# Linear attention into a sine-activated MLP on one core: first loads reordered, weight casts placed by hand, attention steps on one-bank PSUM tiles

## The chip, the cores and the metric

The kernel runs on one core of a Trainium2 chip. The metric is device time in microseconds, the median of several executions. TensorE (PE, with its weight loads PEld) multiplies matrices into PSUM, VectorE (DVE) and ScalarE (ACT) read PSUM and SBUF, GpSimd (POOL) works in SBUF only, and SyncE (SP) issues transfers. Each engine takes its instructions in the order in which the program lists them for it.

## The reference

```python
q_s = softmax(q, axis=-1)                    # per row, 8 batches, 8 heads, 576 x 64
k_s = softmax(k, axis=2)                     # along the sequence
kv  = einsum('bhsd,bhse->bhde', k_s, v)
x   = einsum('bhsd,bhde->bhse', q_s, kv)     # -> x: (4608, 512)
h   = x @ w_in                               # w_in: (512, 2048)
g   = h + sin(alpha * h)**2 / (alpha + 1e-9)
out = g @ w_out                              # w_out: (2048, 512), out: (4608, 512)
```

## The kernel before

Tokens are split in two ways. Attention goes by batch: 8 batches of 576 rows, held as 9 groups (J) of 64. The MLP goes by tile t: 9 tiles of 512 tokens. Tile t needs the attention output (tile `xT`, features on partitions) of batches up to t, except that tile 8 needs batch 7 at most.

A tile is 16 steps `ni`, one for each 128 of the 2048 hidden units. In step ni, `mm_h` runs four matmuls of 512 columns into a PSUM tile `hp` (a ring of four one-bank tiles), and `snake` runs Sin on ACT, the square on ACT ("A"), POOL ("P") or DVE ("D"), and a DVE operation that adds hp and frees its PSUM tile. The second product, `mm_o`, is 64 matmuls for each tile. It runs one tile later: `o_stream(t-1)` feeds some of these matmuls behind each step of tile t, by the count `want`. Four times a tile `evac_o` copies a finished accumulator out and stores it.

Attention of a batch is: `exp_q`, `exp_k` (ACT, two operations each), `cast_v` (two casts to bf16 into `vb`), `norm_q` (DVE row sums and reciprocal, then one multiply into `qn`), `kv_mm` (36 small matmuls of `ke` and `vb` into `kvp`), `kv_norm` (DVE, into `kvb`), three `q_transpose` (six PE transposes into `tp`, one copy into `qT`), and four `attn_out` (two matmuls into `xp`, two copies into `xT`). The tiles kvp, tp and xp share the pool `ps_a`, which has one buffer of two banks. Batches 0 and 1 run on their own, ahead of tile 0 and ahead of tile 1. Batch t+1 is spread over the steps of tile t for t from 1 to 6: exponentials, casts and the loads of the next batch behind step 1, `norm_q` with its multiply on POOL behind step 4, `kv_mm` behind 5, `kv_norm` behind 6, the transposes behind 8 to 10, `attn_out` behind 12 to 15. Each of these stands behind that step's `snake` in program order, so on DVE the copies queue behind the add of the step.

All weights and inputs are float32 in memory and are loaded into a ring of six staging tiles (tag "st"): q, k, v of batch 0, then four chunks of w_in, four of w_out, then the later batches. A chunk of w_in comes as two transfers of 64 partitions, one from SP's queue and one from ACT's. The w_in chunks are cast to bf16 on DVE, one ahead of every fourth step of tile 0 (line 266), behind all adds that were listed earlier. The w_out chunks are cast on POOL behind the whole of tile 0 (line 277). In tile 0 `mm_o` runs on its own, with four accumulators at once.

Of the kernel before, what the change touches and what calls it, by code (L numbers as in the profile page):

```python
# [15 lines left out]
F32 = mybir.dt.float32  # L16
# [7 lines left out]
def kernel(  # L24
# [20 lines left out]
    J = 9  # L45
# [18 lines left out]
    ps_a = ctx.enter_context(tc.tile_pool(name="ps_a", bufs=1, space=bass.MemoryType.PSUM))  # L64
# [40 lines left out]
    def load_win(c):  # L105
        st = stage.tile([128, 4, 512], F32, name="st_w", tag="st")
        for x, eng in ((0, nc.sync), (1, nc.scalar)):
            eng.dma_start(out=st[64 * x:64 * x + 64], in_=win_v[x][:, :, c * 512:(c + 1) * 512])
        wst["i", c] = st
# [61 lines left out]

    def q_transpose(b, g):
# [33 lines left out]
    def snake(t, ni, hp, sq):  # L206
# [174 lines left out]
```

## Time and profile before

| | |
|---|---|
| median of 3 runs | 439.46 us (438.34 to 441.27) |
| profiled execution | 441.32 us, its span 439.0 us |
| mean granted TensorE clock | 0.891 of full speed |
| PE busy | 317.4 us, 72% of the span |
| ACT busy | 232.6 us, 53% |
| DVE busy | 210.1 us, 48% |
| POOL busy | 58.1 us, 13% |

The span is the stretch that the trace covers; 2.3 us of the profiled execution lie around it. Busy shares are averages over stages that differ much, so the rows below go by stage.

### The profile page before, as it was taken

The page shows a single profiled execution, that of the slowest core. Times are in us where ns is not written, and L with a number is a line of the kernel's source. Part 1 is how long each engine was busy: PE and PEld are TensorE (multiplying, and loading weights), DVE is VectorE, ACT ScalarE, POOL GpSimd, SP SyncE. Part 2 cuts the span into 40 slices and gives each one's busy share as a digit, 9 for nine tenths or more (in the row PEclk, how much of TensorE's full clock was granted, in tenths as well). Part 3 has the DMA queues.
Part 4 walks back from the last instruction along what each step waited for, and adds up shares of the span by engine and source line. Part 5 has one row for each costly group of instructions (what it writes and reads, how often), then busy time and mean ns, then how long its engine had stood idle before and what let it go on. Part 6 is the DMA issues. An engine that isn't in the chain of part 4 may idle for free.

```text
span 439.0 us, 4398 instructions
## 1 busy us (share of the span) xinstructions
PE 317.4 (72%) x1621; PEld 147.8 (34%) x1649; DVE 210.1 (48%) x331; ACT 232.6 (53%) x326; POOL 58.1 (13%) x40
## 2 busy tenths in 40 slices
PE   0055566915754689588877969795889588999995
PEld 0032122403322334234333424342434243444442
DVE  0545543073255634554646284628453665554531
ACT  0505337000861459357825974595569456777730
POOL 0000006300213020500140032005000300000000
PEclk9999668965765889899969997997899899999999
DMA  7994234669080001118210911191111111212133
GB/s 262 298 266 167 97 111 166 261 185 342 5 317 1 0 2 23 24 24 276 103 28 16 341 54 24 32 339 25 26 24 25 24 24 26 48 24 50 28 69 72
DMA packets 22821, 46.43 MB, mean 106 GB/s; under 512 B 1792, under 2 KB 1808, under 8 KB 22800
## 3 DMA queue, kind: packets, MB, share of 16 engines
q1 hardware_dynamic: 21712, 44.06, 32.1%
q10 hardware_dynamic: 1088, 2.10, 1.7%
q8 instruction: 13, 0.21, 0.2%
q14 instruction: 8, 0.07, 0.0%
HBM read 36.71 MB, written 9.44 MB: 105 GB/s over the span
## 4 chain that ended last, share of the span: by engine, by line
PE 42%; ACT 21%; DVE 15%; issue 10%; POOL 6%; DMA 2%; POOLq 1%; SPq 0%; ACTq 0%; DVEq 0%
PE hp L202 19%; PE op L219 16%; ACT s L208 9%; POOL qn L144 5%; ACT s L210 4%; DVE g L215 3%; DVE xT L192 3%; PE tp L180 3%; ACT ke L121 3%; DVE qs L141 2%; ACT L121 2%; DMA st_k<-in_k_dram 2%; ACT qe L121 2%; ACT L208 2%; PE hp L219 2%
## 5 line engine op out<-in xcount | busy, mean ns | idle before, releaser
L215 DVE SCALAR_TENSOR_TENSOR g<-s,inva_sb,hp 128x512 bf16<-128x512 f32 x144 | 106.3, 745 | 158.9 <-ACT s L210 139.4
L202 PE MATMUL hp<-xT,win 128*128 128x512 bf16 x569 | 165.7, 422 | 20.0 <-DVE win L266 12.0
L208 ACT ACTIVATE s<-hp,alpha_sb 128x512 f32<-128x512 f32 x144 | 98.2, 684 | 121.4 <-PE hp L202 106.8
L219 PE MATMUL op<-wout,g 128*128 128x512 bf16 x523 | 140.6, 392 | 4.7 <-POOL wout L277 3.8
L202 PEld LDWEIGHTS <-win 128*128 128x128 bf16 x576 | 61.4, 108 | 96.4 <-issue 30.2
L219 PEld LDWEIGHTS <-g 128*128 128x128 bf16 x576 | 57.0, 101 | 73.3 <-issue 15.4
L210 ACT ACTIVATE s<-s 128x512 f32<-128x512 f32 x126 | 79.4, 630 | 4.0
L180 PE MATMUL tp<-identb,qn 128*128 128x128 bf16 x144 | 17.0, 278 | 62.1 <-POOL qn L144 22.0
L144 POOL TENSOR_TENSOR qn<-qe,qs 128x2304 bf16<-128x2304 bf16 x6 | 24.3, 4047 | 171.4 <-ACT s L210 160.6
L180 PEld LDWEIGHTS <-qn 128*128 128x128 bf16 x144 | 13.4, 127 | 72.2 <-DVE qn L144 27.7
L224 DVE COPY o<-op 128x512 f32<-128x512 f32 x34 | 22.9, 676 | 29.4 <-PE op L219 29.4
L188 PE MATMUL xp<-qT,kvb 128*128 128x256 bf16 x64 | 15.2, 324 | 23.7 <-DVE xT L192 19.1
L192 ACT CAST xT<-xp 128x256 bf16<-128x256 f32 (+1 forms) x8 | 2.8, 402 | 51.7 <-PE xp L188 51.7
L141 DVE TENSOR_REDUCE qs<-qe 128x36 f32<-128x2304 bf16 x8 | 20.4, 2546 | 12.3 <-ACT qe L121 12.3
L212 POOL TENSOR_TENSOR s<-s 128x512 f32<-128x512 f32 x10 | 10.4, 1041 | 116.6 <-ACT s L208 116.6
L192 DVE CAST xT<-xp 128x256 bf16<-128x256 f32 (+1 forms) x56 | 22.8, 448 | 5.8 <-PE xp L188 5.8
L188 PEld LDWEIGHTS <-kvb 128*128 128x128 bf16 x64 | 6.6, 106 | 34.6 <-issue 27.1
L121 ACT ACTIVATE qe<-st_q 128x1152 bf16<-128x1152 f32 x16 | 17.7, 1155 | 0.1
L121 ACT ACTIVATE ke<-st_k 128x1152 bf16<-128x1152 f32 x16 | 17.6, 1146 | 0.0
L181 DVE COPY qT<-tp 128x768 bf16<-128x768 bf16 x24 | 13.3, 554 | 8.0 <-PE tp L180 8.0
L121 ACT ACT_TABLE_LOAD x8 | 10.3, 1283 | 11.3 <-DMA st_k<-in_k_dram 11.2
L135 POOL CAST vb<-st_v 128x1152 bf16<-128x1152 f32 x14 | 15.8, 1162 | 0.0
(26 smaller groups left out, 83.3 us busy)
## 6 DMA issues: line engine op xcount, KB each, us to landing
out_dram<-o SPq DMA_DIRECT2D x72, 128.0 KB, 2.4
st_q<-in_q_dram SPq DMA_DIRECT2D x7, 1152.0 KB, 5.6
st_k<-in_k_dram SPq DMA_DIRECT2D x7, 1152.0 KB, 9.2
st_v<-in_v_dram SPq DMA_DIRECT2D x7, 1152.0 KB, 10.3
st_w<-in_moe_w_out_dram SPq DMA_DIRECT2D x4, 1024.0 KB, 8.0
st_w<-in_moe_w_in_dram ACTq DMA_DIRECT2D x4, 512.0 KB, 9.5
st_w<-in_moe_w_in_dram SPq DMA_DIRECT2D x4, 512.0 KB, 16.1
st_q<-in_q_dram SPq DMA_DIRECT2D x2, 576.0 KB, 6.8
```

The lines of the kernel that those rows point to most:

```text
L121: nc.scalar.activation(dst[:, :, ii * 128:(ii + 1) * 128].rearrange("p j (x d) -> p x j d", x=2), src[:, ii::2], AX.Exp)
L141: nc.vector.tensor_reduce(qs, qe3, axis=AXL.X, op=ALU.add)
L144: eng.tensor_tensor(qn.rearrange("p j (i d) -> p (j i) d", i=4), qe3, qs.unsqueeze(2).to_broadcast([128, J * 4, D]), op=ALU.mult)
L180: nc.tensor.transpose(tp[:, jj, ii], qn[:, 3 * g + jj, ii * 128:(ii + 1) * 128], identb)
L188: nc.tensor.matmul(op[:, half, 0:(j1 - j0) * P], kt[:, hp, :], qT[:, j0:j1, ii, e * 64:(e + 1) * 64], start=True, stop=True)
L192: eng(xT[:, hp, c0:c0 + (j1 - j0) * P], op[:, half, 0:(j1 - j0) * P])
L202: nc.tensor.matmul(hp, win[:, ki, ni * 128:(ni + 1) * 128], xT[:, ki, t * MF:(t + 1) * MF], start=(ki == 0), stop=(ki == 3))
L208: nc.scalar.activation(s, hp, AX.Sin, scale=alpha_sb[:, ni:ni + 1])
L210: nc.scalar.activation(s, s, AX.Square)
L215: nc.vector.scalar_tensor_tensor(G[t][:, ni], in0=s, scalar=inva_sb[:, ni:ni + 1], in1=hp, op0=ALU.mult, op1=ALU.add)
L219: nc.tensor.matmul(acc, G[t][:, ni, j * 128:(j + 1) * 128], wout[:, ni, :], start=(ni == 0), stop=(ni == nN - 1))
L224: eng(o, acc)
```

## The change

The first loads all go through SP's queue, in the order q, k, v, the four w_in chunks, the four w_out chunks, batch 1. The w_in casts move to POOL (chunks 0 and 2) and DVE (1 and 3), and three of the four w_out casts move into tile 0. `norm_q` can be done in halves on two engines; for batch 0 both halves go to DVE, for batch 1 one to DVE and one to POOL. `cast_v` of batch 0 moves to POOL. The pool ps_a gets two buffers, and kvp becomes two one-bank tiles, xp one such tile per half. In batches 0 and 1 the copies of the transposes go to ACT, and the two halves of `attn_out` to DVE and ACT. The row sums of batch 1 move ahead of tile 0's output copies. `snake` is split into `sine` and `combine`, and the attention steps of a tile stand between `mm_h` and these. In the tiles the exponentials, `norm_q` and `cast_v`, in this order, stand behind step 0, `kv_mm` and `kv_norm` in step 4, the transposes in 6 to 8, `attn_out` in 9 to 12, and step 0 takes 20 matmuls of `o_stream`.

```diff
-    ps_a = ctx.enter_context(tc.tile_pool(name="ps_a", bufs=1, space=bass.MemoryType.PSUM))
+    ps_a = ctx.enter_context(tc.tile_pool(name="ps_a", bufs=2, space=bass.MemoryType.PSUM))
...
     def load_win(c):
         st = stage.tile([128, 4, 512], F32, name="st_w", tag="st")
-        for x, eng in ((0, nc.sync), (1, nc.scalar)):
-            eng.dma_start(out=st[64 * x:64 * x + 64], in_=win_v[x][:, :, c * 512:(c + 1) * 512])
+        for x in range(2):
+            nc.sync.dma_start(out=st[64 * x:64 * x + 64], in_=win_v[x][:, :, c * 512:(c + 1) * 512])
         wst["i", c] = st
...
-    def norm_q(b, eng):
+    def norm_q(b, engs):
+
         qe = A["qe", b]
-        qs = small.tile([128, J * 4], F32, name="qs")
-        qe3 = qe.rearrange("p j (i d) -> p (j i) d", i=4)
-        nc.vector.tensor_reduce(qs, qe3, axis=AXL.X, op=ALU.add)
-        nc.vector.reciprocal(qs, qs)
         A["qn", b] = qn = att1.tile([128, J, 4 * D], BF16, name="qn")
-        eng.tensor_tensor(qn.rearrange("p j (i d) -> p (j i) d", i=4), qe3,
-                          qs.unsqueeze(2).to_broadcast([128, J * 4, D]), op=ALU.mult)
-
-    def kv_mm(b, ii, first):
-        if first:
-            A["kvp", b] = ps_a.tile([128, 2, 512], F32, name="kvp", tag="a")
+        qs = small.tile([128, J, 4], F32, name="qs")
+        n = len(engs)
+        w = 4 // n
+        for h in range(n):
+            cols = slice(h * w * D, (h + 1) * w * D)
+            src = qe[:, :, cols].rearrange("p j (i d) -> p j i d", i=w)
+            dst = qn[:, :, cols].rearrange("p j (i d) -> p j i d", i=w)
+            part = qs[:, :, h * w:(h + 1) * w]
+            nc.vector.tensor_reduce(part, src, axis=AXL.X, op=ALU.add)
+            nc.vector.reciprocal(part, part)
+            engs[h].tensor_tensor(dst, src, part.unsqueeze(3).to_broadcast([128, J, w, D]), op=ALU.mult)
+
+    def kv_mm(b, ii):
+        if ii == 0:
+            A["kvp", b] = [ps_a.tile([128, 512], F32, name="kvp", tag="a") for _ in range(2)]
         kvp, ke, vt = A["kvp", b], A["ke", b], vb[b % 2]
         for j in range(J):
             for e in range(2):
                 r = slice(64 * e, 64 * e + 64)
-                nc.tensor.matmul(kvp[:, e, ii * 130:(ii + 1) * 130],
+                nc.tensor.matmul(kvp[e][:, ii * 130:(ii + 1) * 130],
                                  ke[r, j, ii * 128:(ii + 1) * 128],
                                  vt[r, j, ii * 130:(ii + 1) * 130],
                                  start=(j == 0), stop=(j == J - 1))
 
     def kv_norm(b):
-        kvp = A["kvp", b]
         A["kvb", b] = kt = kvb[b % 2]
         kvr = small.tile([128, 2, 2], F32, name="kvr")
-        for x in range(2):
-            r = slice(64 * x, 64 * x + 64)
-            src = kvp[r, :, 0:260].rearrange("p e (ii c) -> p e ii c", ii=2)
-            nc.vector.reciprocal(kvr[r], src[:, :, :, x * 65 + 64])
-            nc.vector.tensor_tensor(
-                kt[r].rearrange("p (ii e) c -> p e ii c", e=2)[:, :, :, x * 64:(x + 1) * 64],
-                src[:, :, :, x * 65:x * 65 + 64],
-                kvr[r].unsqueeze(3).to_broadcast([64, 2, 2, D]), op=ALU.mult)
-
-    def q_transpose(b, g):
+        for e in range(2):
+            for x in range(2):
+                r = slice(64 * x, 64 * x + 64)
+                src = A["kvp", b][e][r, 0:260].rearrange("p (ii c) -> p ii c", ii=2)
+                nc.vector.reciprocal(kvr[r, e], src[:, :, x * 65 + 64])
+                nc.vector.tensor_tensor(
+                    kt[r, e::2, x * 64:(x + 1) * 64],
+                    src[:, :, x * 65:x * 65 + 64],
+                    kvr[r, e].unsqueeze(2).to_broadcast([64, 2, D]), op=ALU.mult)
+
+    def q_transpose(b, g, eng):
...
-        nc.vector.tensor_copy(qT[:, 3 * g:3 * g + 3], tp)
-
-    def attn_out(b, hp, eng):
+        eng(qT[:, 3 * g:3 * g + 3], tp)
+
+    def attn_out(b, hp, half, eng):
         ii, e = divmod(hp, 2)
         qT, kt = A["qT", b], A["kvb", b]
-        op = ps_a.tile([128, 2, 512], F32, name="xp", tag="a")
-        for half, (j0, j1) in enumerate(((0, 4), (4, 9))):
-            nc.tensor.matmul(op[:, half, 0:(j1 - j0) * P], kt[:, hp, :],
-                             qT[:, j0:j1, ii, e * 64:(e + 1) * 64], start=True, stop=True)
-        for half, (j0, j1) in enumerate(((0, 4), (4, 9))):
-            c0 = (J * b + j0) * P
-            eng(xT[:, hp, c0:c0 + (j1 - j0) * P], op[:, half, 0:(j1 - j0) * P])
+        j0, j1 = ((0, 4), (4, 9))[half]
+        n = (j1 - j0) * P
+        xp = ps_a.tile([128, 512], F32, name="xp", tag="a")
+        nc.tensor.matmul(xp[:, 0:n], kt[:, hp, :], qT[:, j0:j1, ii, e * 64:(e + 1) * 64],
+                         start=True, stop=True)
+        c0 = (J * b + j0) * P
+        eng(xT[:, hp, c0:c0 + n], xp[:, 0:n])
...
-    def snake(t, ni, hp, sq):
+    def sine(t, ni, hp, sq):
         s = spool.tile([128, MF], F32, name="s")
         nc.scalar.activation(s, hp, AX.Sin, scale=alpha_sb[:, ni:ni + 1])
         if sq == "A":
@@ -212,6 +218,9 @@
             nc.gpsimd.tensor_tensor(s, s, s, op=ALU.mult)
         else:
             nc.vector.tensor_tensor(s, s, s, op=ALU.mult)
+        return s
+
+    def combine(t, ni, hp, s):
         nc.vector.scalar_tensor_tensor(G[t][:, ni], in0=s, scalar=inva_sb[:, ni:ni + 1],
                                        in1=hp, op0=ALU.mult, op1=ALU.add)
...
+    ACT_CP, DVE_CP = nc.scalar.copy, nc.vector.tensor_copy
     nc.sync.dma_start(out=alpha_rows, in_=moe_alpha.rearrange("(no ni) -> no ni", ni=128))
     load("q", q, 0, halves=True)
     load("k", k, 0, halves=True)
     load("v", v, 0, halves=True)
+    for c in range(4):
+        load_win(c)
     make_identity(nc, ident)
-    nc.vector.tensor_copy(identb, ident)
+    DVE_CP(identb, ident)
     for n in range(2):
         nc.vector.memset(vb[n].rearrange("p j (i c) -> p j i c", i=4)[:, :, :, D:D + 1], 1.0)
         nc.vector.memset(kvb[n], 0.0)
-    load_win(0)
-    load_win(1)
-    load_win(2)
+    tpa = ps_a.tile([128, nN], F32, name="tpa", tag="a")
+    nc.tensor.transpose(tpa, alpha_rows, ident[0:nN, 0:nN])
+    DVE_CP(alpha_sb, tpa)
+    nc.vector.reciprocal(inva_sb, alpha_sb)
+
     exp_q(0)
     exp_k(0)
-    norm_q(0, nc.vector)
-    load_win(3)
-    tpa = ps_a.tile([128, nN], F32, name="tpa", tag="a")
-    nc.tensor.transpose(tpa, alpha_rows, ident[0:nN, 0:nN])
-    nc.vector.tensor_copy(alpha_sb, tpa)
-    nc.vector.reciprocal(inva_sb, alpha_sb)
+    norm_q(0, [nc.vector, nc.vector])
+    cast_v(0, nc.gpsimd)
+    for c in range(4):
+        load_wout(c)
     for g in range(3):
-        q_transpose(0, g)
-    cast_v(0, nc.vector)
+        q_transpose(0, g, ACT_CP)
     for ii in range(2):
-        kv_mm(0, ii, ii == 0)
+        kv_mm(0, ii)
     kv_norm(0)
+
+    def cast_win(c, eng):
+        eng(win[:, :, c * 512:(c + 1) * 512], wst["i", c])
+
+    def cast_wout(c, eng):
+        eng(wout[:, 4 * c:4 * c + 4, :], wst["o", c])
+
+    cast_win(0, nc.gpsimd.tensor_copy)
     for hp in range(4):
-        attn_out(0, hp, nc.vector.tensor_copy if hp % 2 == 0 else nc.scalar.copy)
-
-
+        attn_out(0, hp, 0, DVE_CP)
+        attn_out(0, hp, 1, ACT_CP)
+    cast_win(1, DVE_CP)
+
+
+    load_batch(1)
     SQ0 = "APADAPADPADAPADP"
     for ni in range(nN):
-        if ni % 4 == 0:
-            c = ni // 4
-            nc.vector.tensor_copy(win[:, :, c * 512:(c + 1) * 512], wst["i", c])
-            if c < 2:
-                load_wout(c + 2)
-            elif c == 2:
-                load("q", q, 1)
-                load("k", k, 1)
-            else:
-                load("v", v, 1)
         hp = mm_h(0, ni)
-        snake(0, ni, hp, SQ0[ni])
-    for c in range(4):
-        nc.gpsimd.tensor_copy(wout[:, 4 * c:4 * c + 4, :], wst["o", c])
+        if ni == 2:
+            cast_win(2, nc.gpsimd.tensor_copy)
+        if ni == 6:
+            cast_win(3, DVE_CP)
+        if ni in (7, 10, 13):
+            cast_wout(ni // 3 - 2, nc.gpsimd.tensor_copy)
+        combine(0, ni, hp, sine(0, ni, hp, SQ0[ni]))
+    cast_wout(3, nc.gpsimd.tensor_copy)
 
     accs = [ps_o.tile([128, dm], F32, name="op", tag="o") for _ in range(2)]
     accs += [ps_h.tile([128, dm], F32, name="hp", tag="h") for _ in range(2)]
@@ -282,21 +297,20 @@
         for j in range(4):
             mm_o(0, j, ni, accs[j])
     exp_q(1)
+    norm_q(1, [nc.vector, nc.gpsimd])
     exp_k(1)
-    load("q", q, 2)
-    load("k", k, 2)
+    cast_v(1, nc.gpsimd)
     for j in range(4):
-        evac_o(0, j, accs[j], nc.vector.tensor_copy)
-    norm_q(1, nc.vector)
-    cast_v(1, nc.gpsimd)
-    load("v", v, 2)
+        evac_o(0, j, accs[j], DVE_CP)
+    load_batch(2)
     for g in range(3):
-        q_transpose(1, g)
-    kv_mm(1, 0, True)
-    kv_mm(1, 1, False)
+        q_transpose(1, g, ACT_CP)
+    kv_mm(1, 0)
+    kv_mm(1, 1)
     kv_norm(1)
     for hp in range(4):
-        attn_out(1, hp, nc.vector.tensor_copy if hp % 2 == 0 else nc.scalar.copy)
+        attn_out(1, hp, 0, DVE_CP)
+        attn_out(1, hp, 1, ACT_CP)
...
         for ni in range(nN):
             hp = mm_h(t, ni)
-            snake(t, ni, hp, "A" if t > 1 else SQ0[ni])
             if b is not None:
-                if ni == 1:
-                    exp_q(b)
-                    exp_k(b)
-                    cast_v(b, nc.gpsimd)
-                    if b + 1 < B:
-                        load_batch(b + 1)
-                elif ni == 4:
-                    norm_q(b, nc.gpsimd)
-                elif ni == 5:
-                    kv_mm(b, 0, True)
-                    kv_mm(b, 1, False)
-                elif ni == 6:
+                if ni == 4:
+                    kv_mm(b, 0)
+                    kv_mm(b, 1)
                     kv_norm(b)
-                elif 8 <= ni < 11:
-                    q_transpose(b, ni - 8)
-                elif ni >= 12:
-                    attn_out(b, ni - 12, nc.vector.tensor_copy)
+                elif 6 <= ni < 9:
+                    q_transpose(b, ni - 6, DVE_CP)
+                elif 9 <= ni < 13:
+                    attn_out(b, ni - 9, 0, DVE_CP)
+                    attn_out(b, ni - 9, 1, DVE_CP)
+            combine(t, ni, hp, sine(t, ni, hp, "A" if t > 1 else SQ0[ni]))
+            if b is not None and ni == 0:
+                exp_q(b)
+                exp_k(b)
+                norm_q(b, [nc.gpsimd])
+                cast_v(b, nc.gpsimd)
+                if b + 1 < B:
+                    load_batch(b + 1)
             if os is not None:
-                if b is not None:
-                    want = 20 + 16 * ni // 5 if ni >= 1 else 3
-                    want = min(64, want)
-                else:
-                    want = 4 * (ni + 1)
-                while done < want:
+                want = 20 + 11 * ni // 4 if b is not None else 4 * (ni + 1)
+                while done < min(64, want):
                     next(os)
                     done += 1
```

## Rows read from the trace of the kernel before

**Rows 1.** Windows by stage: busy us of each engine (count), granted clock, DMA share, GB/s
```profile
0.00:35.20 35.20, 7.36 (x63) 4.97 (x65) 13.81 (x24) 7.25 (x10) 0.70 (x6) 1.00 0.96 279
35.20:73.40 38.20, 23.21 (x62) 8.29 (x63) 17.86 (x23) 18.94 (x27) 7.06 (x7) 0.78 0.35 117
73.40:89.00 15.60, 15.51 (x63) 6.56 (x63) 0.51 (x1) 2.66 (x3) 7.71 (x5) 0.89 0.62 227
89.00:111.90 22.90, 7.26 (x64) 4.94 (x65) 11.98 (x18) 0.91 (x3) 0.00 (x0) 0.55 0.77 253
111.90:156.80 44.90, 26.36 (x127) 11.58 (x129) 22.55 (x37) 23.63 (x32) 13.32 (x10) 0.73 0.22 79
156.80:365.20 208.40, 169.24 (x935) 80.52 (x949) 110.80 (x183) 137.03 (x190) 29.36 (x14) 0.93 0.24 76
365.20:439.00 73.80, 68.47 (x312) 30.92 (x316) 32.60 (x47) 42.21 (x64) 0.00 (x0) 1.00 0.20 47
```
**Rows 2.** Timeline of PE in tile 4: start, us, instruction, [idle before <- releaser]
```profile
243.31 4.48 PE L219 MATMUL op<-wout,g 128*128 128x512 bf16 x20
...
263.56 0.82 PE L180 MATMUL tp<-identb,qn 128*128 128x128 bf16 x6 [4.40 <-POOL qn L144]
...
276.74 0.41 PE L188 MATMUL xp<-qT,kvb 128*128 128x256 bf16 x2 [1.20 <-DVE xT L192]
...
283.19 0.38 PE L202 MATMUL hp<-xT,win 128*128 128x512 bf16 x1 [0.53 <-DVE xT L192]
```
**Rows 3.** Windows of tile 4, behind its longest PE wait
```profile
263.50:268.40 4.90, 4.84 (x21) 2.63 (x22) 0.83 (x2) 0.96 (x2) 2.21 (x3) 0.50 0.00 0
268.40:275.00 6.60, 6.44 (x35) 3.07 (x34) 3.77 (x6) 4.13 (x7) 0.00 (x0) 0.97 0.17 40
```
**Rows 4.** Timeline of ACT from the start
```profile
0.73 10.40 ACTq L108 DMA_DIRECT2D st_w<-in_moe_w_in_dram  x3
11.16 1.28 ACT L121 ACT_TABLE_LOAD   x1 [11.16 <-DMA st_k<-in_k_dram]
```
**Rows 5.** Timeline of PE, second chunk of w_in in tile 0
```profile
44.87 6.30 PE L202 MATMUL hp<-xT,win 128*128 128x512 bf16 x16 [3.85 <-DVE win L266]
```
**Rows 6.** Timelines of DVE and PE between tiles 0 and 1
```profile
92.28 0.69 DVE L224 COPY o<-hp 128x512 f32<-128x512 f32 x1 [1.91 <-DMA out_dram<-o]
...
98.49 0.82 PE L180 MATMUL tp<-identb,qn 128*128 128x128 bf16 x6 [9.39 <-DVE qn L144]
```
**Rows 7.** The page's DMA issues: count, KB each, median us from issue to landing
```profile
st_q<-in_q_dram SPq DMA_DIRECT2D x2, 576.0 KB, 6.8
```
**Rows 8.** Windows of the first loads (last two columns: DMA share, GB/s)
```profile
6.00:12.00 6.00, 0.00 (x0) 0.00 (x0) 0.00 (x0) 0.84 (x1) 0.00 (x0) 1.00 1.05 390
24.00:30.00 6.00, 2.89 (x39) 2.18 (x39) 3.38 (x8) 0.00 (x0) 0.00 (x0) 1.00 1.08 199
```
**Rows 9.** Groups by line and shape: busy, mean ns of one | idle before it
```profile
L208 ACT ACTIVATE s<-hp,alpha_sb 128x512 f32<-128x512 f32 x144 | 98.2, 684 | 121.4 <-PE hp L202 106.8 <-DVE g L215 13.6 <-PE xp L188 0.5
...
L121 ACT ACTIVATE qe<-st_q 128x1152 bf16<-128x1152 f32 x16 | 17.7, 1155 | 0.1
...
L277 POOL CAST wout<-st_w 128x2048 bf16<-128x2048 f32 x4 | 7.4, 1891 | 0.0
L167 DVE TENSOR_TENSOR kvb<-kvp,kvr 64x256 bf16<-64x256 f32 x16 | 6.8, 422 | 0.5
```
**Rows 10.** Timelines of ACT, DVE and POOL in tile 4
```profile
244.23 0.63 ACT L210 ACTIVATE s<-s 128x512 f32<-128x512 f32 x1
...
246.17 2.22 ACT L121 ACTIVATE qe<-st_q 128x1152 bf16<-128x1152 f32 x2
...
256.33 2.54 DVE L141 TENSOR_REDUCE qs<-qe 128x36 f32<-128x2304 bf16 x1
...
259.46 4.05 POOL L144 TENSOR_TENSOR qn<-qe,qs 128x2304 bf16<-128x2304 bf16 x1 [35.48 <-ACT s L210]
263.45 2.26 POOL L135 CAST vb<-st_v 128x1152 bf16<-128x1152 f32 x2
```

More of the change, by code (lines that the diff above doesn't have):

```diff
@@ L238 @@
         nc.vector.memset(kvb[n], 0.0)
-    load_win(0)
-    load_win(1)
-    load_win(2)
+    tpa = ps_a.tile([128, nN], F32, name="tpa", tag="a")
+    nc.tensor.transpose(tpa, alpha_rows, ident[0:nN, 0:nN])
+    DVE_CP(alpha_sb, tpa)
+    nc.vector.reciprocal(inva_sb, alpha_sb)
     exp_q(0)
     exp_k(0)
-    norm_q(0, nc.vector)
-    load_win(3)
-    tpa = ps_a.tile([128, nN], F32, name="tpa", tag="a")
-    nc.tensor.transpose(tpa, alpha_rows, ident[0:nN, 0:nN])
-    nc.vector.tensor_copy(alpha_sb, tpa)
-    nc.vector.reciprocal(inva_sb, alpha_sb)
+    norm_q(0, [nc.vector, nc.vector])
+    cast_v(0, nc.gpsimd)
+    for c in range(4):
+        load_wout(c)
     for g in range(3):
-        q_transpose(0, g)
-    cast_v(0, nc.vector)
+        q_transpose(0, g, ACT_CP)
     for ii in range(2):
-        kv_mm(0, ii, ii == 0)
+        kv_mm(0, ii)
     kv_norm(0)
-    load_wout(0)
-    load_wout(1)
+    def cast_win(c, eng):
[3 more added lines that the diff above has]
+    cast_win(0, nc.gpsimd.tensor_copy)
     for hp in range(4):
-        attn_out(0, hp, nc.vector.tensor_copy if hp % 2 == 0 else nc.scalar.copy)
+        attn_out(0, hp, 0, DVE_CP)
+        attn_out(0, hp, 1, ACT_CP)
+    cast_win(1, DVE_CP)
+    load_batch(1)
     SQ0 = "APADAPADPADAPADP"
     for ni in range(nN):
-        if ni % 4 == 0:
-            c = ni // 4
-            nc.vector.tensor_copy(win[:, :, c * 512:(c + 1) * 512], wst["i", c])
-            if c < 2:
-                load_wout(c + 2)
-            elif c == 2:
-                load("q", q, 1)
-                load("k", k, 1)
-            else:
-                load("v", v, 1)
-        hp = mm_h(0, ni)
-        snake(0, ni, hp, SQ0[ni])
-    for c in range(4):
-        nc.gpsimd.tensor_copy(wout[:, 4 * c:4 * c + 4, :], wst["o", c])
+        hp = mm_h(0, ni)
+        if ni == 2:
[6 more added lines that the diff above has]
+    cast_wout(3, nc.gpsimd.tensor_copy)
     accs = [ps_o.tile([128, dm], F32, name="op", tag="o") for _ in range(2)]
@@ L307, in o_stream @@
                 if ni == nN - 1:
-                    evac_o(t, j, acc, nc.vector.tensor_copy)
+                    evac_o(t, j, acc, DVE_CP)
                 yield
```

## The prediction

> **What bounds the kernel now.** I cut the span into stages and read the windows first [rows 1]. Tiles 7 and 8 and the last product take 73.8 us, with PE nearly full and its clock at 1.00. The five tiles 2 to 6 take 208.4 us, 41.7 each, at a mean clock of 0.93. Ahead of them lie 156.8 us in which PE is busy for 79.7: attention of batch 0 (to 35.2), tile 0 (38.2), its second product (15.6), attention of batch 1 (22.9), tile 1 (44.9). DVE, ACT and POOL are no fuller there, so these stages are chains of waits, and not one engine's work.
>
> Then the waits in each. In a steady tile PE stops for 4.40 us at the first transposes, until POOL has made qn; for 1.20 us twice in attn_out, because the copies of xp stand behind an add that waits for ACT; and for 0.53 us at the next tile's first product, which waits for the last xT copy [rows 2]. That is 7.33 us. Behind the longest wait the granted clock is 0.50 for 4.90 us with PE busy, then 0.97 [rows 3]: 2.4 us more. So a tile holds 41.7 - 7.3 - 2.4 = 32.0 us of PE work and small gaps. At the start ACT spends 10.40 us issuing its w_in transfers and loads its Exp table only at 11.16 [rows 4]. In tile 0 PE waits 3.85 us for a w_in cast that stands behind the adds of earlier steps [rows 5]; one such wait stands for three. Between tiles 0 and 1 an output copy waits 1.91 us for a store, the row sums stand behind it, and PE stands for 9.39 us until qn [rows 6].
>
> **Part by part.** Start: without the issues ACT is free at once. Half of q lands in 6.8 us beside the w_in transfers that went ahead of it [rows 7]. 576 KB take 1.5 us at the 390 GB/s of the first loads [rows 8], so I put the first half at 6 and the second at 7.5 (bounds 5 and 9). From 6.0, 1.16 for Exp [rows 9]; then four DVE operations of half size, at half of the 2.54 us row sum each (the multiply taken as long, as it has as many elements), with 0.3 for the two reciprocals and handoffs: qn at about 13. From the first transposes to the first MLP matmul batch 1 took 111.9 - 98.5 = 13.4 us [rows 1, 6], on the one buffer. With two, transposes run beside the copy ahead of them, though an ACT copy of 768 takes about 0.87 us (between 0.68 for 512 and 1.16 for 1152 [rows 9]); in attn_out matmul, copy and handoff of one half lie beside the other's, which I take to save 2 us. kv_norm gets eight operations for four: 0.42 us for 256 elements [rows 9] bounds a half-size multiply between 0.21 and 0.42; at 0.29 that is 0.8 us more in all. I take 11 us (9 to 13.4), so tile 0 begins at **24** (22.5 to 26) for 35.2. cast_v of batch 0, on POOL now, hides behind that: three inputs of 1.18 MB at 390 GB/s from about 2.5 us put v at 12, it is cast by 15, kv_mm comes at 16.5.
>
> Tile 0: the w_in casts leave the head of the steps, so the 3.85 us waits go. What is late next is the loads. While transfers of both queues were in flight they came at 390 GB/s; when only SP's 64-partition halves of w_in were left, at 199 [rows 8]. All eight halves go through SP now, so I take 5.25 us a chunk: w_in at 18, 23.5, 29 and 34, w_out at 36.7, 39.4, 42.1 and 44.8, batch 1 at 47.8 to 54. SP also waits for a free staging tile ahead of each of these (k's and v's, then those that the w_in casts free by 20, 25, 31 and 35.5), which in this order comes before the transfer's own turn, so I cost that at nothing; if a cast comes later, all loads behind it move with it. DVE's cast of chunk 3 holds the add of step 6 until 35.5. On POOL the w_out casts (1.89 us each [rows 9]) stand ahead of the squares of steps 8, 12 and 15, and DVE's adds ahead of the PSUM tiles that later steps need: step 8's add near 41, step 12's near 44.5, whose tile the third accumulator takes. So the second product begins at about 45: **21 us** for 38.2. Below, ACT's 16 Sin of 0.684 [rows 9] and its squares bound it at 17; above, I allow 26. The Trainium skill (DMA: Bandwidth & Descriptors, Issuing engines are not separate DMA queues) says that transfers from several engines interleave on the same DMA engines, and that a second issuing queue saves issue time alone. By that rule the move costs no bandwidth, w_in comes at 390 GB/s and tile 0 takes 17 us; the 199 GB/s speak against it.
>
> The second product stays at **15.6** (to 61). Batch 1's exponentials run at 48 to 54, beside it, and the row sums and multiplies no longer stand behind the output copies. They end by 56, cast_v by 58.5: hidden, with 2 us to spare. Transposes follow the product at once; the four copies with their store wait end 4.5 us later, about when kv_mm does. So **10.5 us** (10 to 12) for 22.9. load_batch(2) stands behind the stores on SP and lands by 72 to 78, when tile 1 wants it.
>
> The steady tile. The copies now stand ahead of the add and have two buffers, so the 1.20 and 0.53 us waits go; qn is early, so the 4.40 goes too. But the exponentials' chain still sets a wait, and POOL's order is now multiply, then cast_v; in the order of before the casts of the next batch ran right behind the multiply, a tile ahead of need [rows 10]. Count from the moment PE leaves step 0's product, 243.31 in [rows 2]: Square at 0.9, exp_q 2.9 to 5.1, row sum and reciprocal until POOL starts at 8.2 (3.13 us in [rows 10]), multiply 4.05, cast_v 2.26: 14.5. The first half of kv_mm may go at 13.4, the second at 14.5, and both end at 15.2. PE gets there after 28 + 16 matmuls; 20 take 4.48 us [rows 2], so 44 take 9.6, and kv_mm would have ended at 10.8. That is **4.4 us lost**, with ACT soon idle too, since its next input is queued behind kv_mm on PE. On DVE kv_norm waits with it, the add of step 4 behind that; the ring of four hp tiles covers these. I charge the half clock behind the wait as before, 2.4 (0 to 4). A tile: 32.0 + 4.4 + 2.4 = **38.8** (36.4 to 41), five 194.
>
> Tile 1 has the same kv_mm wait without matmuls of a second product to cover it, and its first POOL square stands behind multiply and cast. PE reaches kv_mm's end about 18 us in, DVE's late adds (the square of step 1 comes at 14.5 + 1, and three adds and kv_norm behind it) cost 5 more, and 8 steps at 1.8 us, my estimate for PE at half clock part of the time, follow: **37.5** (33 to 42) for 44.9.
>
> Sum: 24 + 21 + 15.6 + 10.5 + 37.5 + 194 + 73.8 = 376.4 us of span for 439.0. The profiled execution was 2.3 us longer than its span and 1.9 above the median: **377 us**.
>
> **Rivals.** (1) The kv_mm wait is not there, if the casts run ahead of the multiply or PE comes later: tiles of 32.0, 34 us less, 343. Against it: POOL takes its instructions in order [rows 10]. (2) The attention steps gain nothing: a longer POOL chain or DVE's adds keep tiles at 41.7, 391. For it, the old and the new wait hang on the same POOL multiply; against it, the three smaller waits have lost their cause. (3) Tile 0 stays slow: POOL's casts and DVE's two casts and four squares in it hold each other up. Six waits of up to 1.89 us are 11 us, 388. The trace of before hardly has such operations side by side, so it speaks neither for nor against it. The Trainium skill (SBUF — State Buffer, SBUF: two separate sides) says this would happen: GpSimd and a VectorE operation with two SBUF inputs share a port pair, and the one that comes second stands until the first ends. That speaks against casting on POOL beside DVE. (4) Slower: PE's clock. Behind the kv_mm wait, if the half clock lasted through the rest of each tile, its 32.0 - 10.8 = 21.2 us of work would take 21.2 more instead of 2.4: five times 18.8, 471. It decides from about 30 us at 0.50 in each tile, where the 62 us are eaten. Against it, [rows 3]: after a 4.40 us wait the clock was back in 4.9 us.
>
> **How the numbers follow.** Forecast 0.64, rival 1 0.06, rival 2 0.14, rival 3 0.11, rival 4 0.03, anything else 0.02. All low ends at once give 354, all high ends 401; neither is likely, and the range from 358 to 396 takes in rivals 2 and 3. A measurement of this kernel can tell about 1%, as its three runs lie within 0.7%: faster 0.95, same 0.02, slower 0.03.
>
> **What would show it.** First Exp near 6; tile 0's first product near 24, the second product near 45, tile 1's first product near 72; a PE wait of 4 to 5 us at kv_mm, released by POOL's cast of vb, in each steady tile, a clock of 0.50 behind it, and none at the transposes or attn_out. The forecast is wrong if the tiles' period isn't 38 to 39 us, or if tile 0 is bound by something other than the loads.

## The result, and the profile after

The changed kernel takes 366.7 us (363.95 to 367.3, four runs) for 440.1 of the kernel before: a ratio of 0.832 (95% interval 0.827 to 0.838), faster by about 73 us. The forecast was 377, with a range from 358 to 396. The profiled execution took 367.3 us, its span 365.4. One execution of 1447 us, in the first experiment below, was disturbed and is left out of the times given there.

The windows of the changed kernel, cut where its stages begin, in the columns of [rows 1] (busy us of each engine, granted clock, DMA share, GB/s):

```profile
0.00:23.20 23.20, 8.11 (x63) 4.96 (x65) 10.73 (x25) 9.67 (x12) 5.49 (x9) 1.00 0.95 257
23.20:45.80 22.60, 16.81 (x63) 6.71 (x64) 15.83 (x20) 15.55 (x24) 11.70 (x8) 0.92 1.06 312
45.80:59.60 13.80, 13.75 (x65) 6.24 (x65) 6.97 (x9) 6.40 (x6) 7.21 (x5) 1.00 0.48 179
59.60:69.10 9.50, 5.68 (x63) 3.10 (x63) 5.54 (x16) 3.65 (x7) 0.00 (x0) 0.82 0.68 169
69.10:105.00 35.90, 23.75 (x127) 11.47 (x129) 21.58 (x39) 22.97 (x31) 10.37 (x7) 0.76 0.75 281
105.00:291.90 186.90, 165.53 (x933) 82.13 (x950) 117.36 (x207) 138.15 (x191) 32.33 (x16) 0.92 0.27 84
291.90:365.40 73.50, 68.34 (x313) 30.93 (x316) 32.54 (x46) 42.12 (x64) 0.00 (x0) 0.98 0.20 47
```

The clock of 1.00 in the first row can't be taken as it stands: there 35 matmuls of kv_mm (at 15.59) take 2.10 us, nearly as long as the 2.26 of 36 at a clock of 0.50 in tile 4 below; at 1.00 they take 1.20. Against [rows 1] line by line, with the forecast between:

| stage | before | forecast | after |
|---|---|---|---|
| to the first MLP matmul | 35.2 | 24 | 23.2 |
| tile 0 | 38.2 | 21 | 22.6 |
| its second product | 15.6 | 15.6 | 13.8 |
| attention of batch 1 | 22.9 | 10.5 | 9.5 |
| tile 1 | 44.9 | 37.5 | 35.9 |
| tiles 2 to 6 | 208.4 | 194 | 186.9 |
| tiles 7, 8 and the rest | 73.8 | 73.8 | 73.5 |

The steady tile: PE's timeline, then POOL's, in tile 4 of the changed kernel.

```profile
188.21 1.03 PE L208 MATMUL hp<-xT,win 128*128 128x512 bf16 x4
193.10 2.26 PE L160 MATMUL kvp<-vb,ke 64*128 64x130 bf16 x36 [3.86 <-POOL vb L135]
...
199.80 0.50 PE L186 MATMUL tp<-identb,qn 128*128 128x128 bf16 x6
...
206.88 0.41 PE L195 MATMUL xp<-qT,kvb 128*128 128x256 bf16 x2
...
208.63 0.41 PE L195 MATMUL xp<-qT,kvb 128*128 128x256 bf16 x2
```
```profile
187.89 4.05 POOL L151 TENSOR_TENSOR qn<-qe,qs 128x2304 bf16<-128x2304 bf16 x1 [31.26 <-PE hp L208]
191.88 2.27 POOL L135 CAST vb<-st_v 128x1152 bf16<-128x1152 f32 x2
```

The waits of [rows 2] are gone: no bracket, that is, no wait, stands at the transposes (L186) or at attn_out (L195). One new wait is there, 3.86 us at kv_mm, and its releaser is POOL's cast, which runs right behind the multiply and no longer a tile ahead. kv_mm begins at 193.10, one cast (1.13 us) behind the multiply's end. The windows across that wait and behind it, the clock in the third column from the right:

```profile
189.30:193.10 3.80, 0.00 (x1) 0.00 (x0) 2.25 (x3) 3.71 (x7) 3.80 (x3) 0.84 1.03 382
193.10:198.60 5.50, 5.17 (x43) 3.04 (x44) 2.58 (x9) 0.13 (x2) 1.05 (x1) 0.50 0.03 7
198.60:216.00 17.40, 17.29 (x96) 8.77 (x97) 12.91 (x23) 13.83 (x22) 0.00 (x0) 1.00 0.13 30
```

As in [rows 3], PE works at 0.50 behind the wait, for 5.5 us here, and then at 1.00.

The start and tile 0: ACT's timeline, then PE's, then POOL's around the wait that is left there.

```profile
0.73 1.28 ACT L121 ACT_TABLE_LOAD   x1 [0.73 <-PEq L374]
5.05 1.16 ACT L121 ACTIVATE qe<-st_q 128x1152 bf16<-128x1152 f32 x1 [3.03 <-DMA st_q<-in_q_dram]
```
```profile
31.82 2.75 PE L208 MATMUL hp<-xT,win 128*128 128x512 bf16 x12 [1.27 <-DVE g L224]
...
40.61 5.32 PE L208 MATMUL hp<-xT,win 128*128 128x512 bf16 x15 [2.80 <-DVE g L224]
```
```profile
36.88 1.89 POOL L272 CAST wout<-st_w 128x2048 bf16<-128x2048 f32 x1 [5.01 <-DMA st_w<-in_moe_w_out_dram]
38.73 1.04 POOL L218 TENSOR_TENSOR s<-s 128x512 f32<-128x512 f32 x1
```

Exp starts at 5.05, as q lands, for 12.44 before (the table load of [rows 4], at 11.16, and its 1.28 us). The w_in waits of [rows 5] are gone from tile 0. In their place PE waits 2.80 us before step 12 for an add, that add for step 8's square on POOL, and the square stands behind a cast that waited until 36.88 for its load. The DMA rate in two windows of the changed kernel, to be read against [rows 8]:

```profile
14.00:32.00 18.00, 13.18 (x78) 6.32 (x79) 9.61 (x19) 10.05 (x17) 6.80 (x5) 1.00 1.08 212
34.00:45.00 11.00, 6.95 (x23) 2.51 (x23) 7.66 (x11) 5.75 (x10) 7.07 (x5) 0.85 1.05 387
```

While w_in comes, in 64-partition halves from one queue, the rate is 212 GB/s; with the 128-partition loads behind it, 387. The DMA share reads full in both (1.08 and 1.05), so it doesn't tell the rate.

### The profile page after: what moved, and what is told of

Same layout as the page of the kernel before. It is cut to its first block, busy times and chain, and to the rows that moved or that the text cites. A ratio compares the mean times of both kernels' runs of the same rounds, so it can differ in the third digit from the quotient of the medians.

```text
span 365.4 us, 4429 instructions
## 1 busy us (share of the span) xinstructions
PE 302.0 (83%) x1619; PEld 145.5 (40%) x1649; DVE 210.6 (58%) x358; ACT 238.5 (65%) x332; POOL 67.1 (18%) x45
## 4 chain that ended last, share of the span: by engine, by line
PE 61%; POOL 10%; DMA 9%; DVE 8%; ACT 6%; issue 3%; SPq 1%; POOLq 0%; DVEq 0%
PE hp L208 27%; PE op L228 27%; POOL qn L151 7%; DMA st_w<-in_moe_w_out_dram 6%; DMA st_w<-in_moe_w_in_dram 3%; DVE qs L149 3%; PE kvp L160 3%; POOL vb L135 2%; PE xp L195 2%; DVE g L224 2%; PE hp L228 2%; ACT qe L121 2%; ACT s L214 2%; ACT L121 1%; PE tp L186 1%
## 5 line engine op out<-in xcount | busy, mean ns | idle before, releaser
L208 PE MATMUL hp<-xT,win 128*128 128x512 bf16 x561 | 154.5, 402 | 7.6 <-DVE g L224 6.3
L208 PEld LDWEIGHTS <-win 128*128 128x128 bf16 x576 | 59.2, 103 | 86.2 <-issue 27.1
L151 POOL TENSOR_TENSOR qn<-qe,qs 128x2304 bf16<-128x2304 bf16 (+1 forms) x7 | 26.4, 3773 | 156.3 <-PE hp L208 131.5
L160 PE MATMUL kvp<-vb,ke 64*128 64x130 bf16 x288 | 16.6, 285 | 29.8 <-POOL vb L135 28.5
L149 DVE TENSOR_REDUCE qs<-qe 128x36 f32<-128x2304 bf16 (+1 forms) x10 | 20.7, 2072 | 20.3 <-ACT qe L121 20.3
L233 DVE COPY o<-op 128x512 f32<-128x512 f32 x34 | 22.9, 676 | 15.2 <-PE op L228 15.2
L160 PEld LDWEIGHTS <-ke 64*128 64x128 bf16 x288 | 13.9, 127 | 33.8 <-issue 28.3
L195 PE MATMUL xp<-qT,kvb 128*128 128x256 bf16 x64 | 16.5, 320 | 6.8 <-DVE kvb L173 3.4
L186 PE MATMUL tp<-identb,qn 128*128 128x128 bf16 x144 | 12.7, 230 | 10.3 <-DVE qn L151 9.4
L135 POOL CAST vb<-st_v 128x1152 bf16<-128x1152 f32 x16 | 18.8, 1199 | 10.6 <-DMA st_v<-in_v_dram 10.6
L186 PEld LDWEIGHTS <-qn 128*128 128x128 bf16 x144 | 10.5, 103 | 15.5 <-DVE qn L151 9.7
L172 DVE RECIPROCAL kvr<-kvp 64x2 f32<-64x2 f32 x32 | 5.4, 167 | 18.8 <-PE kvp L160 18.3
L218 POOL TENSOR_TENSOR s<-s 128x512 f32<-128x512 f32 x10 | 10.5, 1054 | 25.1 <-ACT s L214 25.1
L195 PEld LDWEIGHTS <-kvb 128*128 128x128 bf16 x64 | 6.3, 101 | 13.8 <-DVE kvb L173 4.4
## 6 DMA issues: line engine op xcount, KB each, us to landing
st_v<-in_v_dram SPq DMA_DIRECT2D x7, 1152.0 KB, 10.5
```

What stands on the lines that cost most here:

```text
L135: eng.tensor_copy(vv[:, 2 * ii:2 * ii + 2, :, 0:D], staged["v", b][:, ii::2])
L149: nc.vector.tensor_reduce(part, src, axis=AXL.X, op=ALU.add)
L151: engs[h].tensor_tensor(dst, src, part.unsqueeze(3).to_broadcast([128, J, w, D]), op=ALU.mult)
L160: nc.tensor.matmul(kvp[e][:, ii * 130:(ii + 1) * 130], ke[r, j, ii * 128:(ii + 1) * 128], vt[r, j, ii * 130:(ii + 1) * 130], start=(j == 0 ...
L186: nc.tensor.transpose(tp[:, jj, ii], qn[:, 3 * g + jj, ii * 128:(ii + 1) * 128], identb)
L195: nc.tensor.matmul(xp[:, 0:n], kt[:, hp, :], qT[:, j0:j1, ii, e * 64:(e + 1) * 64], start=True, stop=True)
```

## The experiments

All are edits of the changed kernel, in its line numbers. In the theory that they test, the start of the kernel before was bound by ACT's issues and its steady tile by the order of the attention steps; in the changed kernel the loads bound tile 0, and POOL's order costs the wait at kv_mm and the half clock.

**The casts ahead of the multiply.**

```diff
-                norm_q(b, [nc.gpsimd])
                 cast_v(b, nc.gpsimd)
+                norm_q(b, [nc.gpsimd])
```


> Edit: in the tiles cast_v of a batch stands ahead of norm_q on POOL, nothing else. Theory A (the wait at kv_mm is POOL's order, multiply then cast): the casts run a tile ahead again, the 3.86 us wait at kv_mm goes in each steady tile and with it the half clock of some 5.5 us behind it (2.75 us); qn comes about 12.3 us behind step 0's product, PE reaches the transposes at about 13.6, so nothing takes its place. Tile 37.4 to about 31, five of them 30 us less, tile 1 2 to 4 us less: 332 to 338 us. Theory B (the exponentials' chain sets a wait wherever it is met, or ACT or DVE is the next bound): the wait moves to the transposes, tile 36 or more, 358 to 367 us.

336.2 us (335.9 to 337.6, three runs), ratio 0.764 (0.761 to 0.767). The profile below is of one more run of the same kernel:

> The kernel of the first experiment once more, for a profile. Theory A: no wait of PE at kv_mm from tile 2 on, granted clock 1.00 through tiles 2 to 6, tile near 31.5 us, about 336 us. Theory B: a wait at the transposes of 1 us and more in each tile.

334.9 us. PE's timeline in tile 4, POOL's, and a window of the steady tiles:

```profile
175.39 1.20 PE L160 MATMUL kvp<-vb,ke 64*128 64x130 bf16 x36
...
179.95 0.49 PE L186 MATMUL tp<-identb,qn 128*128 128x128 bf16 x6 [0.45 <-DVE kvb L173]
```
```profile
174.11 4.05 POOL L151 TENSOR_TENSOR qn<-qe,qs 128x2304 bf16<-128x2304 bf16 x1 [22.91 <-PE hp L208]
179.37 2.26 POOL L135 CAST vb<-st_v 128x1152 bf16<-128x1152 f32 x2 [1.20 <-DMA st_v<-in_v_dram]
```
```profile
170.00:205.00 35.00, 34.28 (x205) 16.77 (x206) 25.36 (x42) 30.84 (x42) 6.32 (x3) 1.00 0.50 167
```

The cast that runs at 179.37 is the next batch's. kv_mm has no wait, the clock stays at 1.00, and the Exp table loads lie 31.5 us apart (135.87, 167.37, 198.86) for 37.5 in the changed kernel. Nothing larger than some 0.5 us takes the wait's place. Theory A holds: two lines exchanged are worth 30 us, 6.0 in each of five tiles.

**ScalarE's queue again.**

```diff
-        for x in range(2):
-            nc.sync.dma_start(
+        for x, eng in ((0, nc.sync), (1, nc.scalar)):
+            eng.dma_start(
```


> Edit: the second half of each w_in chunk goes through ScalarE's queue again, issued ahead of its Exp; all else as in the changed kernel. Theory A (the issues hold ACT up, and two queues bring w_in at more than 200 GB/s): first Exp at 10 to 12 us for 5.0, first product of tile 0 at 27 to 29 for 23.2, but w_out lands earlier and the 2.8 us wait of tile 0 shrinks: 367 to 370 us. Theory B (the queue makes no difference to bandwidth, only the issue time counts): 4 to 6 us more, 371 to 373 us.

380.1 us, 13 more, and both theories missed the size. ACT's timeline, then its third and its fourth issue, what SP's fourth w_in issue waited for (in total, times, longest), and POOL's second cast of v:

```profile
0.74 20.22 ACTq L108 DMA_DIRECT2D st_w<-in_moe_w_in_dram  x4
20.99 1.28 ACT L121 ACT_TABLE_LOAD   x1 [20.99 <-DMA st_w<-in_moe_w_in_dram]
```
```profile
10.55 0.60 ACTq L108 DMA_DIRECT2D st_w<-in_moe_w_in_dram  x1
20.33 0.63 ACTq L108 DMA_DIRECT2D st_w<-in_moe_w_in_dram  x1
```
```profile
SPq L108 <- POOL vb L135: 1.2, 1, 1.2
```
```profile
19.13 1.17 POOL L135 CAST vb<-st_v 128x1152 bf16<-128x1152 f32 x1 [2.60 <-DMA st_v<-in_v_dram]
```

In this order four issues, and not three, stand ahead of the Exp, and they hold ACT for 20.22 us for the 10.40 of [rows 4]. An issue itself takes 0.6 to 0.7 us. The first three are through at 11.15, as in the kernel before; the fourth begins at 20.33. SP's issue of the other half of this chunk begins at 20.3 too, and its wait is put down to POOL's cast of v, which ends at 20.30. So the fourth waits for a staging tile: q, k, v and three chunks fill the ring of six, and the first tile to come free is v's. In the kernel before the fourth issue stood behind the Exp of q. The w_in transfer that the table load's bracket names isn't what held ACT, which was itself issuing until 20.96. The first MLP matmul comes at 40.45 for 23.2. Tile 0 takes 18.6 us then (to 59.07, where the second product begins), as its weights are there. The mechanism is that of theory A as far as three issues go; I had taken its price from the kernel before, where the queue held one issue fewer, and had overlooked the tile that the fourth needs.

**Two queues, issued late.**

```diff
-    for c in range(4):
-        load_win(c)
     make_identity(nc, ident)
...
     exp_k(0)
+    for c in range(4):
+        load_win(c)
```
with the second halves on ScalarE's queue as above.

> Edit: the second halves of w_in go through ScalarE's queue, but are issued behind its four Exp operations of batch 0. Theory A (64-partition transfers of one queue run at about 210 GB/s, of two queues at once at up to 390, and the loads bound tile 0): w_in is there at about 23 to 25 us for 32.5, the first w_out chunk at about 27 for 36.9, the 2.8 us wait before step 12 goes; the ACT copies of the first transposes start up to 1 us later. Tile 0 18 to 20 us for 22.6, 362 to 364 us. Theory B (the transfers share the same engines, a second queue adds nothing): first w_out chunk at 36 to 37, 366 to 368 us.

363.3 us (361.8 to 366.5), ratio 0.826 (0.823 to 0.830), whose interval touches that of the changed kernel: the total alone does not settle it. The trace does. The window of the loads and POOL's first w_out cast:

```profile
14.00:24.00 10.00, 6.77 (x52) 3.62 (x53) 3.53 (x12) 3.58 (x8) 3.06 (x2) 1.00 1.06 290
```
```profile
32.76 1.89 POOL L272 CAST wout<-st_w 128x2048 bf16<-128x2048 f32 x1
```

290 GB/s for 212, the cast at 32.76 for 36.88, and the second product at 43.8 for 45.8. So the loads did bound tile 0, though only 2.0 of the 4.1 us reach the second product. Two queues bring 290 and not the 390 that I had put in for them: the 390 of [rows 8] was measured while q, k and v, with 128 partitions, were on their way too. The Trainium skill (DMA: Bandwidth & Descriptors, Issuing engines are not separate DMA queues) lets a second queue save issue time only; with these half-partition transfers the trace shows more, 290 for 212.

**The adds first in the tiles** (the steps' order undone, the buffers kept).

```diff
             hp = mm_h(t, ni)
+            combine(t, ni, hp, sine(t, ni, hp, "A" if t > 1 else SQ0[ni]))
             if b is not None:
...
-            combine(t, ni, hp, sine(t, ni, hp, "A" if t > 1 else SQ0[ni]))
             if b is not None and ni == 0:
```


> Edit: in the tiles each step's Sin, square and add are listed ahead of the attention step again, the two one-bank buffers of ps_a stay. Theory A (the place of the copies behind the add made the waits in attn_out): copies end about 3.2 us behind the step's product, PE wants the buffer back after 1.5 to 2.3, so three waits of about 1 us come back in each tile, and a little more at the transposes: tile 39.5 to 41, 377 to 385 us. Theory B (two buffers alone are enough): 364 to 369 us.

380.4 us, ratio 0.862 (0.859 to 0.865): theory A. PE's timeline in attn_out:

```profile
212.27 0.30 PE L195 MATMUL xp<-qT,kvb 128*128 128x320 bf16 x1 [0.73 <-DVE qT L187]
...
213.99 0.69 PE L195 MATMUL xp<-qT,kvb 128*128 128x256 bf16 x2
...
216.42 0.69 PE L195 MATMUL xp<-qT,kvb 128*128 128x256 bf16 x2 [0.23 <-DVE xT L198]
```

A step takes some 2.4 us there for 1.75 (206.88 to 208.63 in the changed kernel's timeline above), and the tiles 39 to 40.5.

**One buffer** (the order kept).

```diff
-    ps_a = ctx.enter_context(tc.tile_pool(name="ps_a", bufs=2, space=bass.MemoryType.PSUM))
+    ps_a = ctx.enter_context(tc.tile_pool(name="ps_a", bufs=1, space=bass.MemoryType.PSUM))
...
-        xp = ps_a.tile([128, 512], F32, name="xp", tag="a")
+        if half == 0:
+            A["xp"] = ps_a.tile([128, 2, 512], F32, name="xp", tag="a")
+        xp = A["xp"][:, half]
```


> Edit: ps_a has one buffer of two banks again, kvp and the two halves of xp lie in one tile; the order of the steps stays as changed. Theory A (in the tiles the order alone keeps the copies out of PE's way, the second buffer counts only where attention runs on its own): 2 to 4 us more in batch 0 and in batch 1 each, tile at most 0.5 more, 370 to 377 us. Theory B (the second buffer is what removed the waits in the tiles): 1 us and more for each attn_out, tile 40 and more, 380 to 388 us.

391.0 us, ratio 0.891 (0.886 to 0.896): more than either theory gave. PE's timeline:

```profile
220.21 0.27 PE L197 MATMUL xp<-qT,kvb 128*128 128x256 bf16 x1
221.08 0.30 PE L197 MATMUL xp<-qT,kvb 128*128 128x320 bf16 x1 [0.60 <-DVE xT L200]
```

In each attn_out the second half's matmul waits for the first half's copy, four times 0.5 to 0.6 us in a tile, which takes 39.4 to 40.6; and the first MLP matmul comes at 28.65 for 23.2. The kernel before listed both matmuls ahead of both copies, so this edit is worse than its single buffer was. The wait of [rows 2] for the copies of the step before does not come back: the first half of each attn_out has no bracket. So the order is not enough with the halves listed one behind the other; whether it is with both matmuls listed first on a single buffer was not run, and is open.

**The tiles as before.** The loop has the old order on the one-bank tiles, the start stays.

```diff
+            combine(t, ni, hp, sine(t, ni, hp, "A" if t > 1 else SQ0[ni]))
...
+                if ni == 1:
+                    exp_q(b)
+                    exp_k(b)
+                    cast_v(b, nc.gpsimd)
...
+                elif ni == 4:
+                    norm_q(b, [nc.gpsimd])
+                elif ni == 5:
+                    kv_mm(b, 0)
...
+                elif 8 <= ni < 11:
+                    q_transpose(b, ni - 8, DVE_CP)
+                elif ni >= 12:
+                    attn_out(b, ni - 12, 0, DVE_CP)
...
+                    want = 20 + 16 * ni // 5 if ni >= 1 else 3
```


> Edit: the loop over the tiles has the order of before again (adds ahead of attention steps, exponentials behind step 1, multiply behind step 4, transposes 8 to 10, attn_out 12 to 15, 3 matmuls of the second product in step 0), on the new one-bank tiles; the start and tile 0 stay as changed. Theory A (the gain of the start and that of the tiles are separate, and the tiles' part comes from the order): tile 41 to 42, 394 to 400 us. Theory B (the two buffers remove the waits in attn_out whatever the order, only the POOL wait comes back): tile 38.5 to 40, 380 to 390 us.

389.0 us, ratio 0.886 (0.881 to 0.891): the total lies in theory B's range, the tile, 40.4 to 41.1, between the two. The waits of PE in it, in total, times, longest, and its windows of tile 1 and of tiles 2 to 6:

```profile
PE tp L186 <- POOL qn L151: 22.0, 5, 4.4
PE xp L195 <- DVE xT L198: 11.0, 12, 1.8
```
```profile
68.10:110.20 42.10, 24.96 (x127) 11.86 (x129) 23.11 (x41) 23.39 (x31) 13.17 (x10) 0.77 0.64 240
110.20:313.00 202.80, 167.77 (x935) 79.46 (x949) 113.59 (x203) 137.05 (x190) 29.60 (x14) 0.94 0.25 78
```

POOL's 4.4 us is back in five tiles, and the two waits in attn_out at 0.80 each (at 224.90 and 229.66 in one of the tiles) for the 1.20 of [rows 2]: the buffers give a third of those, the order the rest. So of the 73 us the order in the tiles brings 22 (389 - 367). The other 51 are not all of the start: up to tile 1 the kernel before takes 111.9 us, this one 68.1, the changed kernel 69.1, some 43. The rest, some 8, is in the tiles even in the old order: 42.1 for 44.9 in tile 1 and 202.8 for 208.4 in tiles 2 to 6, where the one-bank tiles are the main thing that differs from the kernel before.

**The w_out casts last.**

```diff
-        if ni in (7, 10, 13):
-            cast_wout(ni // 3 - 2, nc.gpsimd.tensor_copy)
...
-    cast_wout(3, nc.gpsimd.tensor_copy)
+    for c in range(4):
+        cast_wout(c, nc.gpsimd.tensor_copy)
```


> Edit: the four w_out casts stand on POOL behind all of tile 0's squares, as in the kernel before; all else as changed. Theory A (a cast that waits for its load holds the square of step 8, and with it the adds and PE): the 2.8 us wait of PE before step 12 goes, step 15 ends near 41.5, the second product then waits for the first cast and starts near 44.4 for 45.8: 364 to 366 us. Theory B (casts placed early are what lets the second product start): it starts 2 us later or more, 368 to 372 us.

369.2 us, ratio 0.841 (0.838 to 0.845). PE's timeline:

```profile
36.78 4.59 PE L208 MATMUL hp<-xT,win 128*128 128x512 bf16 x19 [0.55 <-DVE g L224]
45.71 1.01 PE L228 MATMUL op<-wout,g 128*128 128x512 bf16 x2 [4.34 <-POOL wout L272]
```

The 2.80 us wait does go, as theory A had it, and tile 0 ends at 41.4. But the second product waits 4.34 us for the first cast, begins at 45.71 as in the changed kernel, and behind that wait its matmuls run at 0.43 us each until 49.9, for 0.22. So the product takes 16.1 us for 13.8. In the changed kernel the half clock falls into steps 12 to 15 of tile 0 instead, and the product runs at full pace. The total is in theory B's range, but not by B's reason, a later start of the product.

**Both gains together, and tile 1.** The first and the third edit in one:

> Edit: cast_v ahead of norm_q in the tiles and the second halves of w_in on ScalarE's queue behind its Exp, both together. Theory A (they act in different stages and add up): 336.4 of the first and 3.4 less for the second: 331 to 335 us; in the trace no wait at kv_mm, clock 1.00 through the steady tiles, tile near 31 us. Theory B (with the wait gone something else holds a tile, so that an earlier start is lost again): 336 to 340 us.

332.4 us, ratio 0.758 (0.754 to 0.763), and 31.5 us between table loads: they add up. On top of it, in tile 1:

```diff
-            combine(t, ni, hp, sine(t, ni, hp, "A" if t > 1 else SQ0[ni]))
+            combine(t, ni, hp, sine(t, ni, hp, "A"))
```


> Edit: on top of the previous pair (cast_v first, w_in's second halves on ScalarE's queue behind its Exp), tile 1 squares on ACT in all 16 steps, as the later tiles do. Theory A (in tile 1 the square of step 1 stands on POOL behind the multiply of norm_q and holds the adds, a 5.1 us wait of PE before step 5): that wait shrinks to about 1 us, 328 to 330 us for 332.4. Theory B (ACT's nine more squares of 0.63 us make ACT the bound of tile 1): 332 to 336 us.

328.5 us, ratio 0.747 (0.744 to 0.750). PE's timeline in tile 1, first without this edit, then with it:

```profile
83.61 0.58 PE L208 MATMUL hp<-xT,win 128*128 128x512 bf16 x1 [5.09 <-DVE g L224]
```
```profile
76.24 2.27 PE L160 MATMUL kvp<-vb,ke 64*128 64x130 bf16 x36 [5.03 <-POOL vb L135]
...
79.27 2.65 PE L208 MATMUL hp<-xT,win 128*128 128x512 bf16 x6 [0.22 <-issue]
```

The wait for the add is gone; the one left, 5.03 us at kv_mm, ends with the cast of v (in the version without this edit, where PE came later, it was 3.16 us). Tile 1 runs from 68.95 to 97.05 between its table load and the next, 28.1 us for 32.6. This is the fastest version run here, 38 us below the changed kernel.

## Why the prediction was right

**The start** was right in mechanism and size: Exp at 5.05 (forecast 6), first product at 23.2 (24). That the queue held up the Exp is shown by putting it back: three issues hold ACT until 11.15 as before, and the fourth holds it to 20.96 for want of a staging tile. Exp's earlier start is 7.4 of the 12 us. The rest lies in the steps behind it, where the version with one buffer comes 5.4 us later (28.65).

**Tile 0** was right in its bound, the loads, and 1.6 us short: w_in came at 212 GB/s (put in at 199), the first w_out cast began at 36.88 (36.7) and held the square of step 8, as the sum had it. The second product began at 45.8 (45). With its weights there before it began, in the second experiment, tile 0 took 18.6 us, so the loads cost it some 4. What I had not seen is that behind the 2.80 us wait PE has its clock at 0.50, from about 42 to 45, while it makes steps 12 to 15.

**The second product** took 13.8 and not 15.6: it began without a wait and at full pace, where before it began behind a 3.83 us wait, with matmuls at 0.43 us each until 77.7. I had carried the old time over without asking what of it was clock. PE's timeline before:

```profile
73.44 0.59 PE L219 MATMUL op<-wout,g 128*128 128x512 bf16 x2 [3.83 <-POOL wout L277]
...
75.24 1.06 PE L219 MATMUL hp<-wout,g 128*128 128x512 bf16 x2
```

**Batch 1** took 9.5 for 10.5, just below its bounds (10 to 12). Its transposes begin at 59.58, right behind the product and without a wait, so the 9.39 us of [rows 6] are gone; that this is owed to the row sums' new place is read from the trace, and no experiment puts them back. **Tile 1** took 35.9 for 37.5: kv_mm ended 17.1 us into it (18), behind a wait of 8.88.

**The steady tile** went as counted, the wait at kv_mm included (3.86 us), and swapping the casts removes it. Its size missed the prediction's own sign: the period is 36.9 to 37.5 us, and not 38 to 39. The term was too large by 1.3 us in 38.8. With the casts first the tile shows the work with next to no wait: 31.5 us, where I had 32.0; the wait was 3.86 for 4.4; so the half clock is left with 37.5 - 31.5 - 3.9 = 2.1 us for 2.4. Five tiles make 7 of the 11 us by which the sum of the span, 376.4, was long. All its parts but tile 0 were too long, so that little cancelled.

**The rivals.** (1), no wait at kv_mm, did not come about in the changed kernel, but its size was near: with the casts first it is worth 30 us where I had 34. (2) fell: the three smaller waits are gone. Two experiments show that the buffers without the order leave some of them; that the order needs two buffers is shown only for halves listed one behind the other. (3), POOL and DVE holding each other up, is there but small; see below. (4) fell: in tile 4 the clock is back 5.5 us behind the wait, no tile's period is above 37.6, and in tiles without the wait the clock does not fall at all.

Still open: what the second and third issue on ScalarE's queue wait for. They begin at 7.54 and 10.55, when the first halves of q and k have just landed, and the trace shows no more.

## What to carry to other kernels

When a step is moved earlier on an engine, look at what it pushes back on that same engine: here a cast with a tile to spare was put behind a multiply that the critical step of the same tile did not need yet, and gave back 30 us of the gain. When order and buffers change together, try each without the other: here two buffers without the order left waits, and a single buffer left others, inside a step. A wait of some 4 us on PE should be priced with the half clock behind it, here 2 us more. And a DMA issue on an engine that computes can hold it for longer than the issue takes, here 9 us for a staging tile.

## What the runs showed of the hardware

POOL and DVE do hold each other up, in some pairs. DVE's and POOL's timelines in tile 0 of the changed kernel:

```profile
29.18 1.80 DVE L220 TENSOR_TENSOR s<-s 128x512 f32<-128x512 f32 x1
...
35.27 0.68 DVE L220 TENSOR_TENSOR s<-s 128x512 f32<-128x512 f32 x1
...
41.13 1.02 DVE L220 TENSOR_TENSOR s<-s 128x512 f32<-128x512 f32 x1
```
```profile
28.54 1.89 POOL L269 CAST win<-st_w 128x2048 bf16<-128x2048 f32 x1 [0.72 <-DMA st_w<-in_moe_w_in_dram]
...
39.72 1.89 POOL L272 CAST wout<-st_w 128x2048 bf16<-128x2048 f32 x1
```

DVE's square takes 0.68 us alone, at 35.27. The two that begin beside a POOL cast end 0.55 us (30.98) and 0.54 us (42.15) after that cast ends (30.43 and 41.61): they stood until POOL was done. That agrees with the rule of the Trainium skill (SBUF — State Buffer, SBUF: two separate sides) that rival 3 rested on. DVE's adds beside the same casts, with one input in PSUM, took their usual 0.75. The two squares lost 1.12 and 0.34 us, far from the 11 us of that rival, because few pairs met. With two queues more of them meet: there DVE's cast of a w_in chunk, 1.23 us alone, takes 2.24 from 33.49 on, beside POOL's cast (to 34.65), and POOL's square behind it 2.02 for 1.04.
